# Four loads of turned x and of turned exponentials, each over 128 partitions instead of 32

## The chip, the cores and the metric

The kernel runs on one core of a Trainium2 chip. The metric is the device time of one execution in microseconds (us); before the change it is 747.16 us, the median of three runs (742.86 to 752.12).

## The reference

For each of 8 batches and 8 heads, 512 tokens and 32 states of 64 numbers read each other by attention; the 544 rows of all heads side by side (512 numbers) then go through one gated feed-forward layer.

```python
scores = scale * np.matmul(x, state.transpose(0, 1, 3, 2))      # x: 8, 8, 512, 64; state: 8, 8, 32, 64
a = softmax(scores);   xread = np.matmul(a, state)
scores2 = scale * np.matmul(state, x.transpose(0, 1, 3, 2))
a2 = softmax(scores2); sread = np.matmul(a2, x)
x = np.concatenate([xread, sread], axis=2)                      # then (B, H, 544, 64) to (B * 544, H * 64)
xn = x / sqrt(mean(x * x) + 1e-6) * rms_g
out = (silu(xn @ w_gate) * (xn @ w_val)) @ w_out                # 512 to 1536 to 512
```

All of it is in 32-bit floats.

## The kernel before

The batches are worked through one after another. In the period of batch b, TensorE does the feed-forward products of batch b (`hidden_seven` with its matmuls at L868, and `project_twice` with L1172), and between them the attention of batch b + 1: `tokens_read` with `scores`, then `states_read`. A scheme that trades block products for sums of blocks lowers the count of products; the sums keep VectorE (DVE) and GpSimd (POOL) busy, and ScalarE (ACT) copies results out of PSUM.

The order of all this is written out by hand. Each piece of work is a Python generator, one letter stands for one generator, and a string of letters (`PERIOD`, with `FIRST` for batch 1 and `LAST` for batch 7) says which goes on by one step. Every engine executes its instructions in the order in which the string issues them. SP issues most transfers, on DMA queue q1: weights (L214), quarters of output weights (L1117), x (L138), states (L133) and the results (L1288). ACT issues a few on queue q10, among its own copies and activations; those are the ones that matter here.

**Turned x.** For the scores, TensorE needs x with the 64 numbers of a head on the partitions. For batches 0 and 1 TensorE turns it itself. From batch 2 on, `scores` lets VectorE turn blocks of 32 x 32 (L348) into `xB`, writes `xB` to a scratch tensor in DRAM in one transfer of 1 MB (L350), and reads it back in four loads of 256 KB into `xT`, named `xG` in the profile (L355). The scratch tensor and the tile are

```python
x_d = [scratch.tile([4, 4, Ns, 4 * P], F32, name="x_d%d" % k) for k in range(2)]    # q, g, f, (j r)
xT = one.tile([P, 4, 4, P], F32, name="xG", tag="xT")                               # partition (q f), g, j, r
```

with Ns = 32 and P = 128. Partition 32 q + f of group g gets the 512 numbers of `x_d[q, g, f]`. Before, load q takes the 32 partitions of one q, and in each of them all four g. The score matmuls at L365 use 64 partitions of the tile and all 512 columns (g and r) of one j.

**Turned exponentials.** `states_read` does likewise with the exponentials of the second softmax: VectorE turns blocks (L638) into `eB`, one transfer of 512 KB goes to `e_d` (L641), and four loads of 128 KB read it back into `e2T` (L645), which the profile names `e`. `e_d` has the dimensions j, t, g, and 256 numbers; partition 32 g + t of the tile gets for each j the numbers of `e_d[j, t, g]`. Before, load g takes the 32 partitions of one g with all four j. The matmuls at L656 use all 128 partitions of one j at a time.

In both, each load has 128 rows, of 2 KB for x and of 1 KB for the exponentials. The first load of a group waits for the write before it; each load is one step of the generator, so other work of ACT can stand between two loads. Six batches (2 to 7) with two groups of four make 48 loads. After the fourth load the generators go on: in `scores` with the score matmuls (L365), in `states_read` with the reciprocal (L649) and the matmuls at L656.

A transfer of another kind is of use for comparison: `load_state` (L133) reads `state[b, e::2]`, four heads of 32 rows of 64 numbers, into one tile of 128 partitions.

Of the kernel before, what the change touches and what calls it, by code (L numbers as in the profile page):

```python
# [60 lines left out]
def kernel(  # L61
# [20 lines left out]
    nc = tc.nc  # L82
# [3 lines left out]
    Ns = state.shape[2]  # L86
# [39 lines left out]
    def load_state(b):  # L126

        if b:
            rows[b] = two.tile([P, 2, D], F32, name="rows")
        else:  # L130
            rows[b] = x_0.tile([P, 3, D], F32, name="rows_0")
        for e in range(2):
            nc.sync.dma_start(out=rows[b][:, e], in_=state[b, e::2])  # L133
# [57 lines left out]
    x_d = [scratch.tile([4, 4, Ns, 4 * P], F32, name="x_d%d" % k) for k in range(2)]  # L191
    e_d = [scratch.tile([4, Ns, 4, 8 * Ns], F32, name="e_d%d" % k) for k in range(2)]
# [18 lines left out]
    def fetch(n):  # L211

        if NM // 2 <= n < (B + 1) * (NM // 2):
            nc.sync.dma_start(out=new_w(n), in_=w_d[n % (NM // 2)])  # L214
# [107 lines left out]
    def scores(b, packed, soft):  # L322

        xb = x_sb[b]
        stT = one.tile([P, 4, Ns], F32, name="stT")
        tp = aps.tile([P, 4, Ns], F32, name="at")
        TE.transpose(out=tp.rearrange("p j n -> p (j n)"),
                     in_=packed.rearrange("p e d -> p (e d)"), identity=ident)
        yield
        (VE.tensor_copy if b < 2 else SE.copy)(stT, tp)  # L330
        yield "step"

        if b < 2:
            xT = one.tile([P, 4, NC, P], F32, name="xT", tag="xT")
            for c in range(NC):
                tp = aps.tile([P, 4, P], F32, name="at")
                for j in range(4):
                    TE.transpose(out=tp[:, j, :], in_=xb[:, c, P * j:P * j + P], identity=ident)  # L338
                yield
                SE.copy(xT[:, :, c, :], tp)  # L340
                yield "step"
            xT = xT.rearrange("p j c t -> p j (c t)")
        else:


            xB = one.tile([P, 4, 4, NC, Ns], F32, name="xB", tag="xT")
            for q in range(4):
                VE.transpose(out=xB[:, q], in_=xb[:, q // 2::2, :, Ns * (q % 2):Ns * (q % 2) + Ns])  # L348
                yield
            nc.scalar.dma_start(out=x_d[b % 2].rearrange("q g f r -> (g f) q r"),  # L350
                                in_=xB.rearrange("p q j c t -> p q (j c t)"))
            yield
            xT = one.tile([P, 4, 4, P], F32, name="xG", tag="xT")
            for q in range(4):
                nc.scalar.dma_start(  # L355
                    out=xT[Ns * q:Ns * q + Ns].rearrange("f g j r -> f g (j r)"),
                    in_=x_d[b % 2][q].rearrange("g f r -> f g r"))
                yield
            xT = xT.rearrange("p g j r -> p j g r")


        sp = [aps.tile([P, S], F32, name="at") for e in range(2)]
        for j in range(4):
            for e in range(2):
                TE.matmul(out=sp[e][Ns * j:Ns * j + Ns, :], lhsT=stT[D * e:D * e + D, j, :],  # L365
                          rhs=xT[D * e:D * e + D, j],
                          start=True, stop=True)
        yield


        sS = read[b] = one.tile([P, 2, NC, P], F32, name="sS")
        eS = one.tile([P, 2, S // Ns, Ns], F32, name="eS", tag="eS")
        soft.update(st=stT, e=eS, raw=[eS[:, e] for e in range(2)])
        for e in range(2):
            VE.transpose(out=eS[:, e].rearrange("p k n -> p (k n)"),
                         in_=(sp[e] if b < 2 else
                              sp[e].rearrange("p (g c t) -> p g t c", g=4, c=NC)))
            yield
            SE.copy(sS[:, e].rearrange("p c t -> p (c t)"), sp[e])
            yield "step" if e else None  # L380
# [221 lines left out]
    def states_read(b):  # L602

        if b == 0:
            yield from state_scores()
        xb, sS = x_sb.pop(b), read.pop(b)
        e2 = one.tile([P, 4, 2, NC, Ns], F32, name="e2")
        exps = e2.rearrange("p g e c t -> p (g e c t)").rearrange("p (e c s) -> p e c s", e=2, s=P)
        s2 = two.tile([P, 2], F32, name="s2")
        m2 = two.tile([P, 2], F32, name="m2")  # L610
        z2 = two.tile([P, 2], F32, name="z2")
        for e in range(2):
            VE.reduce_max(out=m2[:, e:e + 1], in_=sS[:, e].rearrange("p c t -> p (c t)"),
                          axis=AXX)
            yield
        VE.tensor_scalar(s2, m2, -SCALE, None, op0=ALU.mult)
        yield
        for e in range(2):
            to = exps[:, e] if b < 2 else e2[:, :, e].rearrange("p g c t -> p g (c t)")
            SE.activation(out=to, in_=sS[:, e], func=ACTF.Exp, scale=SCALE,  # L620
                          bias=s2[:, e:e + 1], accum_out=z2[:, e:e + 1])
            yield "step" if e else None

        e2T = e2
        if b < 2:
            flat = e2T.rearrange("p j e c n -> p (j e c n)").rearrange("p (e c s) -> p e c s", e=2, s=P)
            for e in range(2):
                tp = aps.tile([P, NC, P], F32, name="at")
                for c in range(NC):
                    TE.transpose(out=tp[:, c, :], in_=exps[:, e, c, :], identity=ident)  # L630
                yield
                SE.copy(flat[:, e], tp)
                yield "step"
        else:


            eB = one.tile([P, 4, 2, NC, Ns], F32, name="eB", tag="eS")
            VE.transpose(out=eB.rearrange("p g e c n -> p (g e c n)"),  # L638
                         in_=e2.rearrange("p g e c t -> p (g e c t)"))
            yield  # L640
            nc.scalar.dma_start(out=e_d[b % 2].rearrange("j t g f -> (j t) (g f)"),  # L641
                                in_=eB.rearrange("p g e c n -> p (g e c n)"))
            yield
            for g in range(4):
                nc.scalar.dma_start(out=e2T[Ns * g:Ns * g + Ns].rearrange("t j e c n -> t j (e c n)"),  # L645
                                    in_=e_d[b % 2][:, :, g].rearrange("j t f -> t j f"))
                yield
        VE.tensor_scalar(z2, z2, 1e-9, None, op0=ALU.add)
        VE.reciprocal(z2, z2)  # L649
        yield  # L650
        rp = aps.tile([P, 2, D], F32, name="at")
        for e in range(2):
            for c in range(NC):
                for j in range(4):
                    h = 2 * j + e
                    TE.matmul(out=rp[Ns * j:Ns * j + Ns, e, :],  # L656
                              lhsT=(e2T[:, j, e, c, :] if b > 1 else
                                    flat[:, e, c, Ns * j:Ns * j + Ns]),
                              rhs=(xb[:, h, c, :] if b > 1 else xb[:, c, D * h:D * h + D] if b else
                                   xb[:, c // HT, h, c % HT, :]),  # L660
                              start=(c == 0), stop=(c == NC - 1))
        if b == 1:
            load_state(2)
            load_x(2)
        yield
        sr = two.tile([P, 2 * D], F32, name="sr")
        for e in range(2):
            to, z = sr[:, D * e:D * e + D], z2[:, e:e + 1]
            if b < 2:
                VE.tensor_scalar(to, rp[:, e, :], z, None, op0=ALU.mult)  # L670
            else:
                SE.activation(out=to, in_=rp[:, e, :], func=ACTF.Copy, scale=z)
        yield
        tp = aps.tile([P, 4, Ns], F32, name="at")
        TE.transpose(out=tp.rearrange("p j n -> p (j n)"), in_=sr, identity=ident)  # L675
        yield
        (VE.tensor_copy if b < 2 else SE.copy)(xsT[:, :, Ns * b:Ns * b + Ns], tp)
        yield "step"
# [676 lines left out]
    with tc.manual_schedule(**by_hand):  # L1355
# [7 lines left out]
        for b in range(1, B):  # L1363
            h, t, u = hidden_seven(S, weights_of(b), lambda b=b: tokens_of(b), True)
            p, c, k, o = project_twice(b, store_tokens(b))
# [13 lines left out]
            for stream in FIRST if b == 1 else LAST if b + 1 == B else PERIOD:  # L1379
                next(streams[stream])  # L1380
            assert all(next(stream, done) is done for stream in streams.values())
        n = B * (NM // 2)
        h, t, u = hidden_seven(NT, (state_weights, state_sums), state_tokens, True,
                               lambda mp: fetch(n + mp + W_BUFS))
        p, c, k = project_seven(NT, store_states, nc.scalar)
# [34 lines left out]
```

## Time and profile before

| | us |
|---|---|
| median of 3 runs | 747.16 |
| lowest and highest run | 742.86, 752.12 |
| span of the profiled execution, from its first to its last instruction | 740.1 |
| TensorE busy in it | 733.7 |
| VectorE, ScalarE, GpSimd busy in it | 559.6, 364.2, 257.8 |

The profiled execution is known by its span alone; the median of the runs lies 7.1 us above it. The granted clock of TensorE is 1.000 throughout.

The views are read like this. A group of instructions has its line, engine, operation, tiles (out<-in), count, and then times. The view of a tile gives for each line the shortest, median and longest duration in ns, and when the first and the last instruction start in us from the span's start. The DMA view gives packets, megabytes and the time that the packets took, as a share of 16 engines over the window asked for; a load's issue on a queue takes some 0.3 us and says nothing of when its data lands. Windows give an engine's busy time in a stretch.

### The profile page before, as it was taken

The page shows a single profiled execution, that of the slowest core. Times are in us where ns is not written, and L with a number is a line of the kernel's source. Part 1 is how long each engine was busy: PE and PEld are TensorE (multiplying, and loading weights), DVE is VectorE, ACT ScalarE, POOL GpSimd, SP SyncE. Part 2 cuts the span into 40 slices and gives each one's busy share as a digit, 9 for nine tenths or more (in the row PEclk, how much of TensorE's full clock was granted, in tenths as well). Part 3 has the DMA queues.
Part 4 walks back from the last instruction along what each step waited for, and adds up shares of the span by engine and source line. Part 5 has one row for each costly group of instructions (what it writes and reads, how often), then busy time and mean ns, then how long its engine had stood idle before and what let it go on. Part 6 is the DMA issues. An engine that isn't in the chain of part 4 may idle for free.

```text
span 740.1 us, 14214 instructions
## 1 busy us (share of the span) xinstructions
PE 733.7 (99%) x5588; PEld 590.5 (80%) x5588; DVE 559.6 (76%) x943; ACT 364.2 (49%) x620; POOL 257.8 (35%) x360
## 2 busy tenths in 40 slices
PE   8999999999999999999999999999999999999998
PEld 7534444889977997789888997899779987899996
DVE  5765786899947994699569984899469955788862
ACT  4888764564265625473366426562647336511220
POOL 2100004622373128412662237412841267325400
PEclk9999999999999999999999999999999999999999
DMA  8979727883683387608880679338860883063411
GB/s 232 358 274 394 284 113 271 319 303 100 188 317 84 105 287 275 189 6 317 228 295 11 255 203 321 77 96 299 274 183 10 318 233 121 1 224 118 137 50 28
DMA packets 58425, 146.14 MB, mean 197 GB/s; under 512 B 10228, under 2 KB 29176, under 8 KB 51448
## 3 DMA queue, kind: packets, MB, share of 16 engines
q1 hardware_dynamic: 47312, 126.30, 48.8%
q10 hardware_dynamic: 11048, 18.95, 9.3%
q8 instruction: 44, 0.72, 0.4%
q14 instruction: 21, 0.17, 0.1%
HBM read 116.46 MB, written 28.77 MB: 196 GB/s over the span
## 4 chain that ended last, share of the span: by engine, by line
PE 97%; ACT 1%; DMA 1%; DVE 0%; SPq 0%; issue 0%; ACTq 0%
PE f L868 40%; PE f L1172 31%; PE f L971 6%; PE pv L764 6%; PE pv L721 3%; PE at L721 3%; PE f L1034 2%; PE at L656 1%; PE at L447 1%; PE at L365 1%; DMA raw<-in_moe_w_gate_dram 1%; PE at L316 0%; PE at L338 0%; PE pv L562 0%; PE at L630 0%; PE at L675 0%
## 5 line engine op out<-in xcount | busy, mean ns | idle before, releaser
L868 PE MATMUL f<-aT_s,v 128*128 128x256 f32 x504 | 118.6, 381 | 0.0
L868 PEld LDWEIGHTS f<-aT_s,v 128*128 128x128 f32 x504 | 94.9, 190 | 19.0 <-DVE h L1226 4.2
L931 DVE TENSOR_TENSOR g<-g,f 128x512 f32<-128x512 f32 x84 | 55.6, 684 | 63.9 <-PE f L868 35.4
L1200 POOL TENSOR_TENSOR kept<-kept 128x256 f32<-128x256 f32 x28 | 20.8, 744 | 199.6 <-DVE kept L1212 119.6
L868 PE MATMUL f<-aT_t,vs 128*128 128x256 f32 x336 | 86.8, 382 | 0.0
L1185 ACT COPY kept<-f 128x512 f32<-128x512 f32 (+1 forms) x56 | 30.1, 538 | 99.0 <-PE f L1172 99.0
L1172 PE MATMUL f<-w,h 128*128 128x128 f32 x588 | 74.9, 276 | 0.0
L868 PEld LDWEIGHTS f<-aT_t,vs 128*128 128x128 f32 x336 | 62.9, 190 | 13.5 <-issue 4.4
L1172 PEld LDWEIGHTS f<-w,h 128*128 128x128 f32 x588 | 70.0, 192 | 0.4
L922 ACT ACTIVATE hb<-g 128x1024 f32<-128x1024 f32 x42 | 44.5, 1059 | 45.5 <-DVE g L931 45.1
L748 POOL TENSOR_TENSOR vs<-v 128x256 f32<-128x256 f32 x42 | 30.8, 732 | 98.5 <-ACT v L733 98.3
L944 DVE TENSOR_TENSOR hb<-hb,f 128x512 f32<-128x512 f32 (+1 forms) x48 | 31.2, 649 | 26.8 <-PE f L868 26.7
L309 POOL TENSOR_TENSOR ri<-ss,mhalf 128x4 f32<-128x4 f32 (+1 forms) x9 | 8.5, 948 | 108.0 <-ACT ss L397 98.8
L971 PE MATMUL f<-wo,hb 128*128 128x512 f32 x96 | 44.7, 601 | 0.0
L868 PE MATMUL f<-aT_t,v 128*128 128x256 f32 x168 | 43.7, 382 | 0.0
L764 PE MATMUL pv<-aT_s,v 128*128 128x512 f32 x96 | 43.3, 595 | 0.2 <-DVE aT_s L581 0.2
L868 PE MATMUL f<-aT_s,vs 128*128 128x256 f32 x168 | 43.2, 380 | 0.0
L1172 PE MATMUL f<-wo,h 128*128 128x128 f32 x336 | 42.1, 275 | 0.0
L1172 PE MATMUL f<-wo,hb 128*128 128x128 f32 x336 | 42.1, 275 | 0.0
L944 DVE TENSOR_TENSOR hb<-hb,c 128x512 f32<-128x512 f32 (+1 forms) x48 | 37.1, 774 | 5.6 <-ACT hb L922 5.2
L1172 PEld LDWEIGHTS f<-wo,hb 128*128 128x128 f32 x336 | 40.3, 192 | 0.4
L1172 PEld LDWEIGHTS f<-wo,h 128*128 128x128 f32 x336 | 39.8, 192 | 0.0
(230 smaller groups left out, 1593.0 us busy)
## 6 DMA issues: line engine op xcount, KB each, us to landing
w_m<-w_d SPq DMA_DIRECT2D x48, 1024.0 KB
w<-t_d SPq DMA_DIRECT2D x49, 576.0 KB
out_dram<-kept SPq DMA_DIRECT2D x28, 256.0 KB
raw<-in_moe_w_val_dram SPq DMA_DIRECT2D x6, 1024.0 KB
raw<-in_moe_w_out_dram SPq DMA_DIRECT2D x6, 1024.0 KB
w_d<-w_m SPq DMA_DIRECT2D x6, 1024.0 KB
x_b<-in_x_dram SPq DMA_DIRECT2D x6, 1024.0 KB
x_d<-xB ACTq DMA_DIRECT2D x6, 1024.0 KB
```

Source lines behind the costliest of these rows:

```text
L721: TE.matmul(out=pv[e][Ns * j:Ns * j + Ns, :], lhsT=stT_g[b][D * e:D * e + D, j, :], rhs=w[D * e:D * e + D, j].rearrange("p m k f -> p (m k ...
L748: GE.tensor_tensor(out=vs[:, 0], in0=a21, in1=a22, op=ALU.add)
L764: TE.matmul(out=to[0], lhsT=lhs(i, k), rhs=r, start=(i == 0), stop=(i == len(rhs) - 1))
L868: TE.matmul(out=ps[:, i, 0:half], lhsT=l[:, i, :], rhs=r, start=(start and i == 0 and k == 0), stop=(k == len(lhs) - 1), skip_group_check= ...
L922: SE.activation(out=hb[:, 2 * mp:2 * mp + 2, 0:n].rearrange("p m (c t) -> p m c t", c=2), in_=q["g"][:, :, :, 0:half], func=ACTF.Silu if s ...
L931: VE.tensor_tensor(out=to, in0=to, in1=q[ps][:, :, 0:half], op=ALU.add)
L944: VE.tensor_tensor(out=part, in0=part, in1=val, op=ALU.mult)
L971: TE.matmul(out=banks[r], lhsT=hb[:, m, P * r:P * r + P], rhs=wo[:, m, :], start=(m == 0), stop=(m == NM - 1))
L1034: TE.matmul(out=banks[name][:, r, :], lhsT=lhs(k)[:, P * r:P * r + P], rhs=rhs(k), start=(start and r == 0 and k == 0), stop=(k == HM - 1) ...
L1172: TE.matmul(out=to[half][:, slot, :], lhsT=lhs[:, k, :], rhs=rhs[:, k, :], start=(fresh and n in (0, 4) and k == 0), stop=(k == QM - 1), s ...
L1185: SE.copy(of_half(k, i), banks[name][i])
L1200: GE.tensor_tensor(out=k[:, 4:8:3], in0=k[:, 5:6].to_broadcast([P, 2, QD]), in1=k[:, 4:8:3], op=ALU.add)
```

## The change

Each load takes one column group of all 128 partitions in place of all columns of 32 partitions: for x the loop goes over g in place of q, for the exponentials over j in place of g. The bytes, the number of loads, and the rows of a load are as before, and so are the steps of the generators.

```diff
-            for q in range(4):
+            for g in range(4):
                 nc.scalar.dma_start(
-                    out=xT[Ns * q:Ns * q + Ns].rearrange("f g j r -> f g (j r)"),
-                    in_=x_d[b % 2][q].rearrange("g f r -> f g r"))
+                    out=xT[:, g].rearrange("p j r -> p (j r)"),
+                    in_=x_d[b % 2][:, g])
                 yield
...
-            for g in range(4):
-                nc.scalar.dma_start(out=e2T[Ns * g:Ns * g + Ns].rearrange("t j e c n -> t j (e c n)"),
-                                    in_=e_d[b % 2][:, :, g].rearrange("j t f -> t j f"))
+            for j in range(4):
+                nc.scalar.dma_start(out=e2T[:, j].rearrange("p e c n -> p (e c n)"),
+                                    in_=e_d[b % 2][j].rearrange("t g f -> g t f"))
                 yield
```

As written, the x load has 128 rows on the SBUF side and 4 x 32 rows (q, f) on the DRAM side; the load of exponentials has 128 rows on the SBUF side and 4 x 32 rows (g, t) on the DRAM side.

## The prediction

> **What bounds the kernel now.** I read the profile page first, for the engine that sets the end.
>
> ```profile
> span 740.1 us, 14214 instructions
> PE 733.7 (99%) x5588; PEld 590.5 (80%) x5588; DVE 559.6 (76%) x943; ACT 364.2 (49%) x620; POOL 257.8 (35%) x360
> PE 97%; ACT 1%; DMA 1%; DVE 0%; SPq 0%; issue 0%; ACTq 0%
> ```
>
> TensorE (PE) is busy for 733.7 of 740.1 us and holds 97% of the chain that ended last. It works through one list written out by hand, so whatever holds PE for a microsecond makes the end a microsecond later, and there are only 6.4 us of idle time to be won. The three times shown have a median of 747.16 us; this profiled execution's span is 740.1, and the 7.1 us between them I carry over unchanged, as time around the span. About 2% (15 us) is what a measurement of this kernel can tell from no change.
>
> Next, the waits, for any on a DMA, and the windows view from the first load of turned x of batch 3 to the matmul that uses it:
>
> ```profile
> POOL ri L309 <- DMA w<-t_d: 2.4, 1, 2.4
> ```
> ```profile
> 222.00:233.10 11.10, 11.10 (x64) 9.04 (x48) 7.22 (x11) 5.97 (x10) 6.11 (x8) 1.00 0.52 142
> ```
>
> The only DMA wait among the groups is one of POOL. PE is busy for all of the 11.10 us (second figure). So the loads are hidden today, and making them shorter can give PE nothing. What decides is how long each has, and how much longer it can become. The view of tile xG gives, batch by batch (2, 3, 4 and 7), the matmuls that use the four loads of turned x (L365) and the issues of the loads (L355):
>
> ```profile
> L365 PE MATMUL at<-xG,stT x16: 589/589/589, 154.8 to 155.3; 64*32 64x512 f32 x16
> L355 ACTq DMA_DIRECT2D xG<-x_d x4: 309/327/683, 141.0 to 144.5; - x4
> ...
> L365 PE MATMUL at<-xG,stT x16: 589/601/613, 233.1 to 233.6; 64*32 64x512 f32 x16
> L355 ACTq DMA_DIRECT2D xG<-x_d x4: 309/352/445, 222.0 to 225.5; - x4
> ...
> L365 PE MATMUL at<-xG,stT x16: 589/601/613, 313.1 to 313.6; 64*32 64x512 f32 x16
> L355 ACTq DMA_DIRECT2D xG<-x_d x4: 309/354/1145, 302.0 to 306.2; - x4
> ...
> L365 PE MATMUL at<-xG,stT x16: 589/601/613, 553.1 to 553.6; 64*32 64x512 f32 x16
> L355 ACTq DMA_DIRECT2D xG<-x_d x4: 309/410/442, 545.0 to 546.4; - x4
> ```
>
> From the first issue to the use there are 13.8, 11.1, 11.1 and 8.1 us. Batches 5 and 6 I take to be like batch 4. For the turned exponentials (L645, used at L656), batches 2 and 3:
>
> ```profile
> L645 ACTq DMA_DIRECT2D e<-e_d x4: 309/443/445, 192.2 to 193.6; - x4
> L656 PE MATMUL at<-x_b,e x64: 219/219/243, 200.5 to 201.4; 128*32 128x64 f32 x64
> ...
> L645 ACTq DMA_DIRECT2D e<-e_d x4: 309/376/445, 272.4 to 273.9; - x4
> L656 PE MATMUL at<-x_b,e x64: 219/219/243, 282.4 to 283.3; 128*32 128x64 f32 x64
> ```
>
> That is 8.3 and 10.0 us; batches 4 to 7 I take as batch 3.
>
> **The change part by part: what stays.** The bytes, the number of loads (48), the 128 packets of 2 KB (x) or 1 KB (exponentials) in each, the places of the issues in ACT's list and the wait for the write before them are the same. What is new is the order of the dimensions. The outermost dimension of a load was 32 on both sides; now the DRAM side begins with a dimension of 4, and the SBUF side with 128.
>
> **On how many DMA engines a load runs.** The kernel already has a load of the new shape: the state load (L133) goes to 128 partitions and reads DRAM as 4 x 32 rows of 256 B. Two of them are the first work of queue q1. The DMA view of 2.10 to 3.68 us, and then of 545.9 to 551.3 us, which holds the four x loads of batch 7 and nothing else of size:
>
> ```profile
> DMA packets 311, 0.09 MB, mean 57 GB/s; under 512 B 264, under 2 KB 311, under 8 KB 311
> ```
> ```profile
> DMA packets 577, 1.07 MB, mean 197 GB/s; under 512 B 64, under 2 KB 64, under 8 KB 576
> q10 hardware_dynamic: 576, 1.05, 88.3%
> ```
>
> Two state loads are 256 packets of 256 B, yet 264 packets are under 512 B: 8 small ones more, 4 for each load. The four x loads are 512 packets of 2 KB and come with 64 small ones: 16 for each load. I read the small ones as one completion per engine that took part. So today's loads run on 16 engines, and a load whose DRAM side begins with 4 runs on 4. The changed loads should run on 4: 32 packets on each of four engines in place of 8 on each of sixteen, and all four loads of a group on the same four engines.
>
> The Trainium skill has the rule for this ("DMA: Bandwidth & Descriptors", section "Why a DMA increments its semaphore by 16 and not by 1"): a DMA gets the largest number of engines up to 16 that divides the slowest dimension above 1 of both of its sides. By it 32 gives 16 engines and 4 against 128 gives 4; the trace agrees for both shapes.
>
> **What a packet costs.** Three windows: the second x load of batch 7 as it begins (546.55 to 546.90), the rest of its group (546.95 to 550.8), and the exponentials of batch 3 in full flow (276 to 277):
>
> ```profile
> q10 hardware_dynamic: 60, 0.12, 91.1%
> ```
> ```profile
> DMA packets 458, 0.82 MB, mean 213 GB/s; under 512 B 58, under 2 KB 58, under 8 KB 458
> q10 hardware_dynamic: 458, 0.82, 100.3%
> ```
> ```profile
> DMA packets 203, 0.19 MB, mean 195 GB/s; under 512 B 28, under 2 KB 202, under 8 KB 202
> q10 hardware_dynamic: 202, 0.18, 88.4%
> ```
>
> 91.1% of 16 engines over 0.35 us is 5.1 us for 60 packets: 85 ns for 2 KB. In the second, 61.8 us for 400 packets: 154 ns. In the third, 14.1 us for 174: 81 ns for 1 KB, and half of 85, 43, is its lower bound. So after a short burst sixteen engines that all write into 32 partitions slow one another to about half. Four engines with 32 partitions each of four different groups stand nearer to the fast row; I take 95 ns and 48 ns, and keep 85 to 154 and 43 to 81 for the range. A group then takes 128 packets x 95 = 12.2 us for x (10.9 to 19.7) and 6.1 us for exponentials (5.5 to 10.4), since all 128 packets of an engine come one after another.
>
> Here a rule speaks for the change: the Trainium skill ("SBUF — State Buffer", section "Door 1: The DMA port swizzle") lets 32 neighbouring partitions reach 8 of 16 ports and 128 all of them. The 154 against 85 ns agree with it. With 16 engines kept, it would halve the group; since nothing waits for it, the sum would be nought.
>
> **The x loads, on the path.** Landing = first issue + 1.0 to 1.2 us until packets flow (545.0 against the window from 545.9) + 12.2 + 0.2 for completion + what queue q1 moves on the same engines meanwhile, packet about packet. For that, q1 in 303.1 to 306 and in 142 to 154.8:
>
> ```profile
> q1 hardware_dynamic: 41, 0.20, 29.0%
> ```
> ```profile
> q1 hardware_dynamic: 545, 3.14, 64.4%
> ```
>
> - Batch 7: 545.0 + 1.0 + 12.2 + 0.2 = 558.4, wanted at 553.1: PE waits 5.3 us.
> - Batch 3: 222.0 + 1.2 + 12.2 + 0.2 = 235.6 against 233.1: 2.5.
> - Batch 4: 302.0 + 1.2 + 12.2 + 0.2 = 315.6, and q1's remainder: 29% x 2.9 x 16 = 13.5 us of packets, 0.8 us each if all engines share it, 3.4 if four do. I take 2: 317.6 against 313.1, 4.5. Three such batches: 13.5.
> - Batch 2: 141.0 + 1.1 + 12.2 + 0.2 + 8.2 (64.4% of 12.8) = 162.7 against 154.8: 8, rounded.
>
> Sum 29.3 us. All of it is on the path: the score matmuls need every column of xG, so they need all four loads, and PE's list has nothing to run in their place. Late next is all that stands behind them in the list; SP's fetches wait for PE and move along.
>
> **The exponentials.** The windows 194.6 to 201 and 274.6 to 282.4 hold all 576 packets of a group, so the flow begins no earlier; beside them stands q1:
>
> ```profile
> q1 hardware_dynamic: 458, 0.97, 46.5%
> q10 hardware_dynamic: 576, 0.52, 40.5%
> ```
> ```profile
> q1 hardware_dynamic: 457, 0.97, 41.5%
> q10 hardware_dynamic: 576, 0.52, 28.0%
> ```
>
> Batch 2: 194.6 + 6.1 + 0.2 + about 2 of q1's 3.0 us (46.5% of 6.4) = 202.9 against 200.5: I take 2. Batch 3: 274.6 + 6.1 + 0.2 + 1.8 (of 3.2) = 282.7 against 282.4: 0.3 to 0.4, five times: 2. Together 4 us.
>
> **Issue on ACT, and queue q1.** The state loads' issues against today's:
>
> ```profile
> L133 SPq DMA_DIRECT2D rows<-in_state_dram x16: 529/562/1887, 0.7 to 456.6; - x16
> L645 ACTq DMA_DIRECT2D e<-e_d x24: 309/445/1381, 192.2 to 594.4; - x24
> ```
>
> An issue may take 0.1 to 0.2 us more, 5 to 10 us over 48. I cost it at nothing: ACT is idle half of the time, and a PE delay of that kind ahead of L365 or L656 shortens the wait there. Without that cover it is up to 10 us. A q1 packet on the four engines waits for at most one packet of a load; a weight fetch of eight 8 KB packets per engine lands about 0.8 us later. No wait of PE for a fetch shows today, so this is nothing too.
>
> **A cold TensorE.** The same kind of matmul at the start of the span:
>
> ```profile
> 1.05 3.78 PE L1312 MATMUL f<-wake 128*128 128x256 f32 x8 [1.05 <-DVE wake L155]
> 9.48 1.95 PE L1312 MATMUL f<-wake 128*128 128x256 f32 x8
> ```
>
> Eight take 3.78 us at first and 1.95 later: after idleness PE runs at half speed for some 4 us and loses up to 1.9. I charge it once, for the longest wait (batch 2): 1.9. Bounds: 0, and 12 x 1.9 = 23.
>
> **Sum:** 29.3 + 4 + 1.9 = 35 us. Span 740.1 + 35 = 775; time 747.2 + 35 = 782. With the low prices (85 and 43 ns, 0.8 us of q1, nothing cold) it is 4.0 + 1.2 + 6 + 6.4 + 1 = 19, hence 766; the likeliest case's own range is 765 to 800.
>
> **The rivals.**
>
> 1. *The loads keep 16 engines: not slower.* Place: how the DMA is split. A load of 8 packets per engine at 85 ns takes 0.7 us and lands ahead of today's; PE waits for nothing before or after: 747. It decides from 8 engines on (64 x 85 = 5.4 us; 222.0 + 1.2 + 5.4 is 4.5 us ahead of use). For it: two equal counts of 128 could be cut anew. Against it: the state load, with the same two shapes, shows 4 completions. Chance 0.12.
> 2. *The four engines still write in one another's way*, in pairs whose partitions lie 32 apart: 154 and 81 ns. Each x group then takes 7.5 us more (45), each exponential group 4.3 (26): 782 + 71 = 853. For it: the slow rows above. Against it: they are of sixteen engines in one group of partitions. Chance 0.12.
> 3. *Most waits leave PE cold.* Eleven more charges of 1.9: 803. For it: the start of the span. Against it: nearly all forecast waits are 0.4 to 5 us, and the trace has none of that length behind which to see it. The Trainium skill ("TensorE: Matmul & The Clock Gate", section "HAM oscillation — how this bites in real kernels") sets the point at gaps of about 3.4 us; no run here shows it. Chance 0.14.
> 4. *Faster by over 2%*: 15 us out of 6.4 us of idle PE time. Chance 0.02.
>
> **How the numbers follow.** The forecast has 0.60. Slower by over 2% (above 762): it, rivals 2 and 3, less 0.01 for its low tail: 0.85. Within 2%: rival 1 and that tail: 0.13. Faster: 0.02. The range goes from 760, just under the low sum, to 850, where rival 2 lies at the edge; rival 1 stays outside.
>
> **What would show it.** The page's row for ACT's queue:
>
> ```profile
> q10 hardware_dynamic: 11048, 18.95, 9.3%
> ```
>
> Right: small packets on q10 fall by 12 for each of 48 loads, 576 in all, from 11048 to 10472; the x group's packets run on for 11 to 13 us at about a quarter of 16 engines; a wait of PE for xG of 2 to 8 us appears at L365 six times, small ones at L656; the span between other places is unchanged. Wrong: 11048 packets as before (rival 1); a mean packet near 154 ns (rival 2); L868 groups after a wait at twice their time (rival 3); or waits of PE elsewhere, for fetches or for ACT's copies, which I cost at nothing.

## The result and the profile after

The changed kernel takes 815.97 us (median of four runs, 813.58 to 818.07) against 745.19 us for the kernel before in the same comparison: the ratio is 1.0945, with a 95% interval of 1.0882 to 1.1008. It lies 71 us above the kernel before; the forecast was 782, the range 760 to 850.

The profile page after, with TensorE's busy time, the chain that ended last, and ACT's DMA queue:

```profile
span 814.6 us, 14201 instructions
PE 750.1 (92%) x5588; PEld 595.6 (73%) x5588; DVE 560.8 (69%) x943; ACT 363.6 (45%) x620; POOL 258.7 (32%) x360
q10 hardware_dynamic: 10472, 18.94, 6.5%
PE 64%; DMA 26%; DVE 4%; ACTq 2%; ACT 2%; issue 1%; SPq 0%; DVEq 0%
```

The chain now runs through DMAs for 26%, and TensorE (PE) is idle for 64.5 us (814.6 - 750.1) where it was idle for 6.4. It is also busy for 16.4 us longer with the same 5588 matmuls. The small packets on q10 fell by 576, to 10472: 12 fewer for each of 48 loads, so each load ran on 4 engines.

The waits of PE after the change (sum, times, longest):

```profile
PE at L365 <- DMA xG<-x_d: 44.4, 6, 18.4
PE at L656 <- DMA e<-e_d: 9.6, 7, 2.6
PE f L868 <- ACT g L920: 3.7, 4, 1.1
```

Together 57.7 us; with the 16.4 us of longer matmuls that is 74.1 of the 74.5 us by which the span grew. Six waits for turned x, the exponentials, a few us of waits for ACT's copies, and a slower TensorE: each has a part of its own below.

Batch 4 shows how a wait looks. First the DMA view of 342.5 to 354.3 us, which holds its four x loads, and of 346 to 352 inside it; then PE's timeline (start, length, instructions, idle time before and what ended it), and the windows view of 3.4 us from the end of the wait on, with a like window of batch 5 that begins 0.4 us before its wait ends (the second column is PE's busy time; the one of the granted clock is third from the end):

```profile
q10 hardware_dynamic: 528, 1.05, 24.6%
```
```profile
DMA packets 305, 0.60 MB, mean 100 GB/s; under 512 B 11, under 2 KB 11, under 8 KB 305
q10 hardware_dynamic: 305, 0.60, 26.2%
```
```profile
348.01 1.89 PE L868 MATMUL f<-aT_s,v 128*128 128x256 f32 x8
354.87 1.80 PE L365 MATMUL at<-xG,stT 64*32 64x512 f32 x16 [4.97 <-DMA xG<-x_d]
356.32 2.07 PE L721 MATMUL pv<-w_m,stT_g 64*32 64x512 f32 x16
```
```profile
354.90:358.30 3.40, 3.40 (x32) 0.81 (x32) 1.59 (x3) 0.00 (x0) 0.00 (x0) 0.53 0.00 0
443.90:447.30 3.40, 2.96 (x32) 0.76 (x32) 0.92 (x2) 0.00 (x0) 0.00 (x0) 0.50 0.00 0
```

The four loads are 528 packets: 512, and four completions for each of the four loads. They keep a quarter of the DMA busy (24.6%), four engines out of sixteen, for 11.6 us. Inside, 26.2% of 16 engines over 6 us is 25.2 us for 294 packets of 2 KB: 86 ns each, the fast price. PE waits 4.97 us, and then runs with a granted clock of 0.5 for 3.4 us: the sixteen score matmuls take 1.80 us where they took 1.09.

### The profile page after: what moved, and what is told of

Its sections match the earlier page's. It is cut to its first block, busy times and chain, and to the rows that moved or that the text cites. A ratio compares the mean times of both kernels' runs of the same rounds, so it can differ in the third digit from the quotient of the medians.

```text
span 814.6 us, 14201 instructions
## 1 busy us (share of the span) xinstructions
PE 750.1 (92%) x5588; PEld 595.6 (73%) x5588; DVE 560.8 (69%) x943; ACT 363.6 (45%) x620; POOL 258.7 (32%) x360
## 3 DMA queue, kind: packets, MB, share of 16 engines
q10 hardware_dynamic: 10472, 18.94, 6.5%
## 4 chain that ended last, share of the span: by engine, by line
PE 64%; DMA 26%; DVE 4%; ACTq 2%; ACT 2%; issue 1%; SPq 0%; DVEq 0%
PE f L868 23%; PE f L1172 17%; DMA xG<-x_d 11%; DMA e<-e_d 7%; DMA x_d<-xB 6%; PE f L971 5%; PE pv L764 5%; PE pv L721 3%; PE f L1034 2%; PE at L721 2%; PE at L365 1%; ACTq L645 1%; DMA e_d<-eB 1%; DVE xB L348 1%; PE at L656 1%
## 5 line engine op out<-in xcount | busy, mean ns | idle before, releaser
L922 ACT ACTIVATE hb<-g 128x1024 f32<-128x1024 f32 x42 | 44.4, 1058 | 46.4 <-DVE g L931 46.0
L365 PE MATMUL at<-xG,stT 64*32 64x512 f32 x96 | 11.6, 1040 | 44.4 <-DMA xG<-x_d 44.4
L944 DVE TENSOR_TENSOR hb<-hb,f 128x512 f32<-128x512 f32 (+1 forms) x48 | 31.1, 649 | 29.3 <-PE f L868 29.1
L915 ACT COPY g<-f 128x512 f32<-128x512 f32 x42 | 24.3, 580 | 47.5 <-PE f L868 42.2
L375 DVE STREAM_TRANSPOSE eS<-at 128x512 f32<-128x512 f32 x14 | 9.8, 709 | 47.5 <-PE at L365 47.5
```

The source lines that it names most:

```text
L915: SE.copy(gates(q)[0], q["x"][:, :, 0:half])
L922: SE.activation(out=hb[:, 2 * mp:2 * mp + 2, 0:n].rearrange("p m (c t) -> p m c t", c=2), in_=q["g"][:, :, :, 0:half], func=ACTF.Silu if s ...
L944: VE.tensor_tensor(out=part, in0=part, in1=val, op=ALU.mult)
```

## The experiments

All are compared with the kernel before on the same chip: 742.5 us beside x_only, e_only, k16 and awake, 742.3 us beside the others.

### One group at a time: x_only and e_only

The change to one of the two loops is undone (the code is shortened).

```diff
 x_only:  -  for j in range(4):  e2T[:, j]              <- e_d[b % 2][j], "t g f -> g t f"
          +  for g in range(4):  e2T[Ns * g:Ns * g + Ns] <- e_d[b % 2][:, :, g], "j t f -> t j f"
 e_only:  -  for g in range(4):  xT[:, g]               <- x_d[b % 2][:, g]
          +  for q in range(4):  xT[Ns * q:Ns * q + Ns]  <- x_d[b % 2][q], "g f r -> f g r"
```

> Only the loads of turned x are changed; the loads of exponentials are as before. Theory (four engines carry a load; each late group holds TensorE, and each long wait leaves it cold): the six waits for xG stay near the 44 us of the changed kernel, with about 13 us of slow TensorE behind them: 797 to 805 us. Rival (the waits for exponentials let the other engines run ahead, and it is that which makes the x groups late): the waits of batches 3 to 6 fall from 5 to about 2.5 us each, so 775 to 790 us.

> Only the loads of exponentials are changed. Theory: six waits at L656 of about 1.6 us, 10 us in all, too short to leave TensorE cold, and a few us of copies behind them: 755 to 761 us. Rival (the two groups compete with each other): nothing is late when x loads are short, 745 to 749 us.

Measured: x_only 786.03 us, ratio 1.0586 (1.0568 to 1.0604), 43.5 us more; e_only 754.85 us, ratio 1.0167 (1.0137 to 1.0196), 12.3 us more. e_only lies 0.15 us below the range of its theory. PE's waits in x_only, then in e_only:

```profile
PE at L365 <- DMA xG<-x_d: 32.3, 5, 18.9
PE at L365 <- issue: 2.3, 1, 2.3
```
```profile
PE at L656 <- DMA e<-e_d: 7.4, 6, 2.0
```

x_only missed its theory and fell where the rival put it. One wait is 18.9 us as before, but those of batches 3 to 6 are 2.3 to 3.1 us in place of 5. The two parts add up to 56 us, the whole change costs over 70: some 15 us come only when both are there. The timeline of ACT's and SP's DMA issues around the write of turned x (L350) says where. Batch 4 in the kernel before, in x_only, in e_only, and in the changed kernel:

```profile
296.13 0.39 ACTq L350 DMA_DIRECT2D x_d<-xB  x1
297.35 1.19 SPq L214 DMA_DIRECT2D w_m<-w_d  x1
302.04 0.31 ACTq L355 DMA_DIRECT2D xG<-x_d  x1
```
```profile
322.58 0.39 ACTq L350 DMA_DIRECT2D x_d<-xB  x1
323.81 1.21 SPq L214 DMA_DIRECT2D w_m<-w_d  x1
328.49 0.53 ACTq L355 DMA_DIRECT2D xG<-x_d  x1
```
```profile
299.65 0.38 ACTq L350 DMA_DIRECT2D x_d<-xB  x1
300.04 0.42 SPq L214 DMA_DIRECT2D w_m<-w_d  x1
308.72 0.32 ACTq L355 DMA_DIRECT2D xG<-x_d  x1
```
```profile
332.85 0.37 ACTq L350 DMA_DIRECT2D x_d<-xB  x1
333.09 0.42 SPq L214 DMA_DIRECT2D w_m<-w_d  x1
341.29 0.53 ACTq L355 DMA_DIRECT2D xG<-x_d  x1
```

The first load waits for the write. In x_only, as before the change, SP issues its 1 MB weight fetch (L214) 1.2 us after the write, and the load follows the write by 5.9 us. In e_only the fetch is issued 0.4 us after it, and the write takes 9.1 us; in the changed kernel it is 0.2 us, and 8.4. In e_only x loads are short, so nothing is late; with the changed x loads it takes away what slack is left. The step is not sharp: in batch 3 the fetch comes 0.5 us behind the write in both x_only and e_only, and the write takes 5.9 us in one and 8.7 in the other.

### The write ahead of the weight fetch: sync_write

```diff
-            nc.scalar.dma_start(out=x_d[b % 2].rearrange("q g f r -> (g f) q r"),
+            nc.sync.dma_start(out=x_d[b % 2].rearrange("q g f r -> (g f) q r"),
```

> The changed kernel, with the write of turned x issued on SP's queue, where it stands ahead of the next weight fetch. Theory (waits for exponentials let SP issue that fetch 1 to 1.6 us earlier against the write, the two share the engines, and the write lands 2.5 to 4 us later): the write takes 5 to 6 us in batches 3 to 6 again, their waits for xG fall from 5.2 to about 2.5 us, and most of them are too short to leave TensorE cold: 794 to 803 us. Rival (the write is slow for another reason): 812 us or more.

Measured: 793.09 us, ratio 1.0691 (1.0652 to 1.0730), 0.9 us below the range of its theory. The timeline around the write of batch 4, and PE's waits:

```profile
324.37 0.37 SPq L350 DMA_DIRECT2D x_d<-xB  x1
324.79 1.93 SPq L133 DMA_DIRECT2D rows<-in_state_dram  x2
326.81 0.84 SPq L214 DMA_DIRECT2D w_m<-w_d  x1
330.27 0.53 ACTq L355 DMA_DIRECT2D xG<-x_d  x1
```
```profile
PE at L365 <- DMA xG<-x_d: 28.4, 5, 18.5
PE at L365 <- issue: 2.5, 1, 2.5
```

With the fetch 2.4 us behind it, the write takes 5.9 us again with both changes in place, and the waits for xG fall from 44.4 to 30.9 us. The edit also gives the write another queue; but in x_only the write is as short on ACT's queue, so that is not what shortens it. It is the fetch beside the write that holds the write up, and it costs 19 us (by the ratios, 1.0945 less 1.0691) to 23 us (by the times) of what the change costs, slower clock included. Not all of this comes from the waits for exponentials. In batch 7 the write took 9.0 us before the change and 8.6 us in x_only; here it takes 5.9, the wait falls from 5.2 to 2.4 us and the clock stays up behind it. That is some 5 us; what is left is near the 15 us that come only when both loops are changed.

### Sixteen engines and 128 partitions: k16 and k16_e

The scratch tensors get an order in which the rows of a load lie at equal steps in DRAM, so its DRAM side has one dimension of 128. The write before it then has to be made in four parts of 32 partitions. k16_e does so for the exponentials alone and leaves x as before the change. In short form:

```diff
-  x_d: [4, 4, Ns, 4 * P];  one write "q g f r -> (g f) q r";  load g from x_d[:, g]
+  x_d: [4, Ns, 4, 4 * P];  for g: x_d[:, :, g], "q f r -> f q r" <- xB[Ns * g:Ns * g + Ns]
+                           load g from x_d[:, :, g], "q f r -> (q f) r"
-  e_d[j, t, g];  one write;  load j from e_d[j], "t g f -> g t f"
+  e_d[g, t, j];  for j: e_d[:, :, j], "g t f -> t g f" <- eB[Ns * j:Ns * j + Ns]
+                           load j from e_d[:, :, j], "g t f -> (g t) f"
```

> All 128 partitions are kept as the target of each load, but the scratch tensors are laid out so that the DRAM side of a load is 128 equally spaced rows; the write before it is made in four parts of 32 partitions. Theory (the number of engines decides, not the partitions): 16 completions for each load, packets of 2 KB at about 85 ns in place of 139 to 158, the four x loads done 3 us after the packets begin, no wait of TensorE: 743 to 749 us. Rival (spreading a load over 128 partitions is itself slow, or rows 8 KB apart are): waits stay, 790 us or more.

> x loads as before the change; the loads of exponentials go to 128 partitions with 128 equally spaced rows on the DRAM side, after a write in four parts. The version for both had no wait for a load, but its x write in four parts took 11 us in place of 6 and held ACT. Theory (128 partitions on 16 engines are harmless, and the 13 us that were left came from the x write): 741 to 746 us, against 755 with the four-engine loads of exponentials. Rival (something in the 128-partition loads or the write in parts costs of itself): 748 to 756 us.

Measured: k16 756.06 us, ratio 1.0181 (1.0166 to 1.0196); k16_e 744.30 us, ratio 1.0037 (1.0004 to 1.0069). k16 missed its 743 to 749 us, though not by the rival; k16_e came out as its theory had it. k16's PE waits, the issues around the x write of batch 4, and the DMA view of the four loads behind it (311.2 to 315.8); then the same view for the kernel before (302.9 to 310.6):

```profile
PE f L870 <- ACT g L922: 10.1, 7, 1.9
```
```profile
299.01 3.21 ACTq L351 DMA_DIRECT2D x_d<-xB  x4
...
310.35 0.34 ACTq L356 DMA_DIRECT2D xG<-x_d  x1
```
```profile
q10 hardware_dynamic: 576, 1.05, 71.8%
```
```profile
q10 hardware_dynamic: 576, 1.05, 63.1%
```

No wait for a load is left. 576 packets are 16 completions per load again, and 71.8% of 16 engines over 4.6 us is 103 ns a packet, against 152 in the kernel before: packets into all 128 partitions with 16 engines take a third less time than those into 32 (the 154 ns of the prediction, from batch 7, were measured with queue q1 still). What is left of 13 us stands, by the trace, at the write in four parts: it takes 11.3 us in place of 5.9, ACT stands waiting for it ahead of the first load, and PE waits 10.1 us for ACT's copies. In k16_e, whose write in four parts takes no longer than the one write did (2.2 to 2.9 us against 2.7 to 3.3), nothing of the kind appears, and the kernel is 0.4% slower than the one before where the four-engine loads cost 1.7%. So neither 128 partitions nor rows at equal steps make a load late. No run has the new loads of turned x behind an undivided write, so that the 13 us are the write's is argued, not shown.

### Two engines: x_k2

Only the x loads are changed, and each is cut into two of 64 partitions (shortened):

```diff
-  for g in range(4):                     xT[:, g]                      <- x_d[b % 2][:, g]
+  for g in range(4):  for q in (0, 2):   xT[Ns * q:Ns * q + 2 * Ns, g] <- x_d[b % 2][q:q + 2, g]
```

> As the kernel with only the x loads changed (786 us), but each load is cut into two of 64 partitions, whose DRAM side begins with a dimension of 2. Theory (the leading dimension sets the number of engines): 2 completions for each of 48 loads, 256 packets one after another on each of two engines, 21.5 us a group at 84 ns; each of the six waits grows by 10.8 us, and the short waits of batches 3 to 6 become long enough to leave TensorE cold: 848 to 860 us. Rival (the number of partitions, or the bytes in a partition, sets the time): 775 to 795 us.

Measured: 849.51 us, ratio 1.1430 (1.1404 to 1.1455), 63 us more than x_only. The page's q10 row, the two longest entries of PE's waits, and the issues of the loads:

```profile
q10 hardware_dynamic: 10760, 18.94, 6.8%
```
```profile
PE f L869 <- ACT g L916: 39.5, 6, 8.4
PE at L366 <- DMA xG<-x_d: 14.3, 8, 3.3
```
```profile
L356 ACTq DMA_DIRECT2D xG<-x_d x48: 489/861/5007, 144.1 to 649.2; - x48
```

10760 is x_only's number too: twice the loads with half the completions, 2 each. The time came out as expected, but not by the way that was written down. Most of it is not at the score matmuls: an issue takes up to 5.0 us, and PE waits for the copies that stand behind it on ACT. That ACT is held because the two engines have too much in their queues is my reading of it. PE's busy time is 32 us longer than in x_only (774.2 against 742.1), as the clock is low behind more waits (a mean of 0.944 against 0.978).

### TensorE kept busy: awake and awake2

```diff
+        for _ in range(0 if b < 2 else 74 if b == 2 else 20):        # awake2: 42 and 11
+            TE.matmul(out=sp[0][:, 0:2 * P], lhsT=wake, rhs=wake.unsqueeze(1).to_broadcast([P, 2, P]),
+                      start=True, stop=True)
         for j in range(4):
             for e in range(2):
                 TE.matmul(out=sp[e][Ns * j:Ns * j + Ns, :], lhsT=stT[D * e:D * e + D, j, :],
```

> The changed kernel, with matmuls on constants put ahead of the score matmuls: 74 in batch 2, 20 in each of batches 3 to 7 (0.24 us each when warm), whose result is overwritten. They fill the waits for xG and add nothing else. Theory (after a wait TensorE runs at half clock for about 3.4 us): the waits become work, the clock stays at 1.0 behind them, and 9 to 12 us of the 16 us of added busy time go: 804 to 808 us. Rival (the added busy time is records of matmuls that wait, not a slow clock): 815 us or more.

> As awake, with 42 matmuls ahead of the score matmuls in batch 2 and 11 in batches 3 to 7, since one took 0.43 us there, not 0.24, and the first version outlasted the waits by 31 us. Theory (slow clock after each wait for xG): the waits are filled and no longer, 804 to 809 us, against 816 for the changed kernel. Rival (no cold TensorE): 815 us or more.

Measured: awake 837.73 us, ratio 1.1293 (1.1261 to 1.1324); awake2 802.23 us, ratio 1.0799 (1.0782 to 1.0817). awake missed both of its ranges and tells little: its matmuls outlasted the waits. In awake2 they fit, and it fell 1.8 us below the range of its theory. The kernel with 97 matmuls more (194 instructions) is 11 us (by the ratios) to 14 us (by the times) faster than the changed kernel. PE's wait for xG, and the windows view of the 3.4 us behind the score matmuls' start in batch 4:

```profile
PE at L368 <- DMA xG<-x_d: 1.7, 4, 0.5
```
```profile
346.80:350.20 3.40, 3.39 (x39) 1.92 (x40) 2.22 (x4) 0.28 (x1) 0.00 (x0) 1.00 0.00 0
```

The clock is 1.00 where the changed kernel had 0.53, and 39 matmuls fit into the 3.4 us that held 32. So the slow clock behind the waits for xG costs 11 to 14 us of the 71. Two small things are in that figure: in batch 3 the write was short again (5.8 us), which is worth 0.5 us, as the added matmuls fill the rest of the wait; and one wait for exponentials is followed by a slow clock here where two are in the changed kernel, some 2 us.

## Why the prediction was right or wrong

**Four engines.** Right, to the packet: the state load's 4 completions carried over, and x_k2's 2 and k16's 16 bear out that the leading dimension of the DRAM side decides. Rival 1 falls with it.

**The price of a packet.** Taken as 95 ns, it was 86. Rival 2's 154 ns did not come: the pairs of engines did not hold one another up. That sixteen engines slow each other in 32 partitions was read from loads of one kind alone; k16's 103 ns in 128 partitions bears it out.

**The x loads, 29.3 us forecast, 44.4 measured.** Batch 7 (5.3 forecast, 5.2 measured) is well sized: PE could go on 13.6 us after the first issue, where I had 13.4; the cheaper packets were made up for by more time before and behind the data. Batches 4 to 6 (4.5 against 5.0 to 5.3) look well sized by chance. The 2 us that I gave to q1 did not come: in batch 4 PE could go on 13.6 us after the first issue, not 15.6. But the write before the loads, which I left at its length, grew from 5.9 to between 8.4 and 9.8 us, so that PE came for the data 8.6 us after the first issue, not 11.1. Batch 3 went from 2.5 to 5.2 by the same write. I had said that SP's fetches move along with PE; the fetch of batch 4, 0.2 us behind the write in place of 1.2, shows that they came earlier than that, and sync_write what it costs. The large miss is batch 2, 8 against 18.4. The term at fault is what queue q1 moves meanwhile, in the DMA view after the change (142.8 to 173.4 us):

```profile
q1 hardware_dynamic: 1153, 6.55, 61.6%
q10 hardware_dynamic: 528, 1.05, 11.4%
```

61.6% of 30.6 us is 18.8 us of q1's packets, as the mean of the engines; I had 8.2, counted to the time at which PE used to need the data. The surplus of 10.6 us is about the miss of 10.4. PE's wait begins at 155.5 us; the same row from 142.8 to 155.5, and from there to 173.4:

```profile
q1 hardware_dynamic: 714, 3.99, 88.3%
q1 hardware_dynamic: 439, 2.56, 42.7%
```

11.2 us of q1's packets lie ahead of the wait (88.3% of 12.7), where the x loads, now on four engines, leave q1 more of the time than they did. The other 7.6 us (42.7% of 17.9) lie in the wait: SP issues one more fetch at 162.0 us, while PE stands.

**The exponentials, 4 us forecast, 9.6 measured.** The same term, as far as batch 3 shows (1.8 us waited, 0.3 to 0.4 forecast): from 309.4 to 318.7 q1 took 4.3 us, as the mean of the engines (45.7% of 9.3), where I took 1.8.

```profile
q1 hardware_dynamic: 520, 1.27, 45.7%
```

**Issue on ACT.** Costed at nothing, it was 3.7 us, and not through longer issues: ACT stands at the first load until the write has landed, later than before, and copies wait behind it. In sync_write, where the write is short again, none of this wait is left.

**A cold TensorE, 1.9 us forecast, 16.4 us of longer busy time measured.** This is the step that failed most, for its size. The price per wait was about right, and the count was wrong: I charged one wait of twelve. The trace after shows the clock at 0.5 behind eight: all six waits for xG, five of which are only 5 us long, and two of those for exponentials (batches 2 and 5, of 2.6 and 2.0 us):

```profile
225.70:228.50 2.80, 2.80 (x49) 2.63 (x40) 0.55 (x1) 0.99 (x3) 0.00 (x0) 0.50 0.19 14
498.70:501.50 2.80, 2.80 (x22) 1.32 (x7) 0.00 (x0) 1.08 (x5) 1.09 (x2) 0.50 0.61 174
```

16.4 us over eight waits is 2.05 us each, and awake2 shows that the clock is what costs it. How long PE stands does not decide alone. In x_only the wait of 2.4 us in batch 5 was followed by the low clock, and the longer one of 3.1 us in batch 6 was not:

```profile
425.70:429.20 3.50, 3.50 (x27) 1.65 (x6) 3.08 (x5) 0.00 (x0) 0.00 (x0) 0.51 0.00 0
509.40:512.90 3.50, 3.50 (x40) 1.99 (x41) 2.34 (x4) 0.40 (x1) 0.00 (x0) 1.00 0.02 5
```

So gaps well below the 3.4 us that rival 3 quotes can lower the clock here; which of them do, no run explains. Rival 3, to which I gave 0.14, describes this part better than the forecast, though its 803 lacks the other misses.

All of these misses have one sign: 35 us became 71, and 816 lies beyond the 765 to 800 that I gave the likeliest case. The stated range held it by luck, because its upper end came from rival 2, which did not occur.

Not tried: why SP is a microsecond early. Its fetch stands behind a store that waits for GpSimd, and GpSimd has no wait for a load; that fits, but no run here changed it alone.

## What to carry to other kernels

Look at the outermost dimension of both sides of a transfer: 4 against 128 gave 4 DMA engines here, 32 or 128 on both sides gave 16, and counting the small packets of a queue tells which. When a hidden transfer comes to light, price it with all that other queues will move until it lands, with the work before it once the engines are out of step, and with a clock that drops: here it dropped behind every wait of about 5 us or more, and behind some of 2 to 3 us. Spreading over all 128 partitions does make packets cheaper (103 against 152 ns), if the rows can be given one dimension of 128. No run here became faster by it, as nothing waited for the loads before, and the write in parts that it needed cost time for turned x.

## What the runs showed of the hardware beyond that

In the changed kernel the first two loads of a group of turned x were issued in 0.5 to 0.6 us each, and the fourth, with up to 96 packets of the group ahead of it on an engine, in 0.8 to 2.4 us:

```profile
L355 ACTq DMA_DIRECT2D xG<-x_d x24: 514/531/2387, 141.4 to 613.3; - x24
```

In x_k2, with eight loads of 32 packets on each of two engines, issues took up to 5.0 us. So the issuing engine began to be held with about 100 packets in an engine's queue; this is an estimate from these two runs, and none varied the depth of the queue alone.
